# Half of one batch's queries transposed by a DMA instead of TensorE, and two scalars loaded from another queue

## The chip, the core and the metric

The kernel runs on one core of a Trainium2 chip. A core has five engines that run side by side and meet through semaphores: TensorE (PE in the profile; its weight loads are the rows PEld), VectorE (DVE), ScalarE (ACT), GpSimd (POOL) and SyncE (SP). Data comes and goes by DMA. Here GpSimd issues every load that turns float32 into bfloat16, and SyncE issues the rest: plain loads, stores, and DMAs that transpose.

The metric is the device time of one execution in microseconds. Before the change it is 219.6 (median of three runs, 218.88 to 221.15).

## The reference

Two parts follow each other: a block attention whose keys and values are mixed by a Sinkhorn-normalised matrix, and a feed-forward layer with a squared ReLU.

```python
# q, k, v: [4, 8, 768, 64]; sort_net: [4, 8, 8, 8]; 8 blocks of 96 tokens
P = sort_net
for _ in range(5):
    P = exp(P - max(P, -1));  P = P / sum(P, -1);  P = P / sum(P, -2)
k_sorted = einsum('bhij,bhjcd->bhicd', P, blocks(k))     # the same for v
attn = softmax(q_block @ k_sorted_block.T / sqrt(64))     # 96 x 96 a block
x = (attn @ v_sorted_block)  -> [3072 tokens, 512]

h = x @ w_in                                              # [512, 2048]
g = s * relu(h) ** 2 + b                                  # s, b scalars
out = g @ w_out                                           # [2048, 512]
```

## The kernel before

The work goes by batch (4) and by half batch (4 blocks of 96, 384 tokens, called TG); there are 8 half batches, t = 0 to 7. For each half batch and each pair of heads (hp = 0 to 3), `s_piece` or `s_banks` makes the scores and their exponential (tile `at`), `p_piece` multiplies by the values and divides (`x`), and `t_piece` (TensorE) or `t_dma` (a transposing DMA) turns `x` into `xt`. Then `ffn1` makes eight column groups (i = 0 to 7, 256 columns of w_in each): matmuls with w_in (L542, tile `hps`), ReLU on ScalarE (L556), the square on VectorE (L557). `ffn2` multiplies by w_out (L568, tile `ops`), and `store` (L593, L596) applies s and the bias and writes out. The bias, b times the column sums of w_out, is made once in `make_bias`: sixteen matmuls (L646, tile `cps`), four steps on VectorE (L648, L651), three copies on GpSimd (L654). No output can be stored before it.

The order on each engine is written by hand: the instructions of an engine run in the order of the program text (`manual_schedule`). `ffn1` and `ffn2` take dictionaries of slots: after column group i, or after a quarter of an output tile, the functions in that slot are emitted, so that attention of the next half or batch lies between the matmuls of the feed-forward layer.

What matters here is the beginning, where weights, keys, values and queries of the first two batches are loaded while the first half batches are computed.

- **GpSimd's queue** (L149 to L183): queries of batch 0, half 0 (`load_qh(0, 0)`, L106); keys of batch 0; then w_in in pieces (L142): four column groups c = 0 to 3 of 256 columns, each as four loads of 64 KB, and two groups of 512 columns as four loads of 128 KB each, used by the column groups 4 and 5, and 6 and 7; before c = 3 stand the queries of batch 0, half 1, as four loads (`load_qh(0, 1, 4)`, L167). Then w_out (L175), values of batch 1 (L95), some memsets, s and b (L181), keys of batch 1, and five of the eight row loads of batch 1's queries (L117). The three copies of the bias follow, and the last three row loads.
- **Queries of batch 0** come as `qh`: tokens as 64 groups of six, each group of a head a contiguous run of 384 numbers. `q_banks` transposes them on TensorE, 48 transposes of 64 x 64 for a half (L228, tile `tqb`), and ScalarE and VectorE move them into `qt` (L214, L216). The tokens of such a `qt` lie in the order (c, t), six apart, so the scores are written permuted and the exponential (L467) puts them back. `q_banks(0, 0)` runs before the first scores; `q_banks(0, 1)` stands in slot 0 of `ffn1(0)` (`QF0`, L694), and the first scores of half 1 (`SB(0)`, L462) in slot 2.
- **Queries of batches 1 to 3** come as rows of tokens (`load_q_rows`, tile `qtok`: 96 tokens on partitions, one load a block, runs of 64 numbers) and are transposed by a DMA on SyncE's queue (`q_dma`, L525), one for each half. Nothing is permuted then.
- The tiles `qh` and `qtok` share two buffers (tag rawq), the two kinds of `qt` share two others (tag qt).
- In `ffn2(0)` the keys of batch 1 are sorted (L328, tile `tpp`) and moved out of PSUM by VectorE and ScalarE (L216, L214, tile `ks`), and the values of batch 1 likewise (L378, tile `tvp`).

Of the kernel before, what the change touches and what calls it, by code (L numbers as in the profile page):

```python
# [10 lines left out]
BF = mybir.dt.bfloat16  # L11
AF = mybir.ActivationFunctionType
# [10 lines left out]
def kernel(  # L23
# [12 lines left out]
    nc = tc.nc  # L36

    B, H, S, D = q.shape
    NB = sort_net.shape[-1]
    BLK = S // NB  # L40
    BH = B * H
    NHP = H // 2
# [3 lines left out]
    HB = NB // 2  # L46
# [3 lines left out]
    KR = GAP + C2  # L50
# [3 lines left out]
    scale = float(D) ** -0.5  # L54
# [6 lines left out]
    trp = ctx.enter_context(tc.tile_pool(name="trp", bufs=2))  # L61
# [11 lines left out]
    CQ = 6  # L73
# [6 lines left out]
    for c in range(0, C2, CV):  # L80
        nc.sync.dma_start(out=v0f[:, c:c + CV, :].rearrange("p c d -> p (c d)"),
                          in_=raw[2][0][:, c * D:(c + CV) * D])
# [3 lines left out]
    def load(t, b, parts=1, behind=None, rest=None):  # L86
        ti = rawp.tile([128, C2, D], BF, tag=f"raw{t}", name=f"raw{t}")
        RAW[t, b] = ti
        if behind is not None:
            nc.gpsimd.tensor_copy(out=ti[0:behind.shape[0], 0, 0:1], in_=behind)  # L90
        n = C2 // parts
        for c in range(0, C2, n):
            if rest is not None and c == 2 * n:
                after(rest)
            nc.gpsimd.dma_start(out=ti[:, c:c + n, :].rearrange("p c d -> p (c d)"),  # L95
                                in_=raw["qkv".index(t)][b][:, c * D:(c + n) * D])
# [3 lines left out]
    def load_qh(b, half, parts=1):  # L100
        if b not in QH:
            QH[b] = rawp.tile([128, H, CQ, D], BF, tag="rawq", name="qh")
        qv = q[b].rearrange("h (f p c) d -> f p h (c d)", f=2, c=CQ)
        for h in range(0, H, H // parts):
            hs = slice(h, h + H // parts)
            nc.gpsimd.dma_start(  # L106
                out=QH[b][half * 64:(half + 1) * 64, hs].rearrange("p h c d -> p h (c d)"),
                in_=qv[half][:, hs])

    QTOK = {}  # L110

    def load_q_rows(b, ns=range(NB)):
        if b not in QTOK:
            QTOK[b] = rawp.tile([BLK, NB, H, D], BF, tag="rawq", name="qtok")
        qv = q[b].rearrange("h (n t) d -> t n h d", n=NB)
        for n in ns:
            nc.gpsimd.dma_start(out=QTOK[b][:, n], in_=qv[:, n])  # L117
# [4 lines left out]
    KS = [const.tile([128, NG, 2, GAP], BF, name=f"ks{i}") for i in range(2)]  # L122
# [17 lines left out]
    def load_wi(f0, f1, al=None):  # L140
        al = slice(0, NHP) if al is None else al
        nc.gpsimd.dma_start(out=wi[:, al, f0:f1], in_=wiv[:, al, f0:f1])  # L142

    def fill_vs(i):
        nc.gpsimd.memset(VS[i][:, :, D:VW], 1.0)
        nc.gpsimd.memset(VS[i][32:GAP, :, D:VW], 0.0)
        nc.gpsimd.memset(VS[i][32:C2, :, D:VW], 1.0)
# [10 lines left out]
    s_bc = const.tile([128, 1], FP)  # L158
    b_bc = const.tile([128, 1], FP)
# [3 lines left out]
    W4 = d_ff // 4  # L163
    W8 = d_ff // 8
    for c in range(4):
        if c == 3:
            load_qh(0, 1, 4)  # L167
        for a in range(NHP):
            load_wi(c * W8, (c + 1) * W8, slice(a, a + 1))
    for c in range(2, 4):  # L170
# [6 lines left out]
    nc.gpsimd.memset(VP[1][:, :, C2:GAP], 0.0)  # L177
    nc.gpsimd.memset(KS[1][:, :, :, C2:GAP], 0.0)
    fill_vs(1)
    for t, src in ((s_bc, moe_s), (b_bc, moe_b)):  # L180
        nc.gpsimd.dma_start(out=t, in_=src.to_broadcast([128, 1]))  # L181
    load("k", 1, 6)
    load_q_rows(1, range(NB - 3))  # L183

    rstat = const.tile([BH, NB], FP)
    rrec = const.tile([BH, NB], FP)
# [20 lines left out]
        else:  # L207
            eng.tensor_copy(out=o, in_=i)

    QT = {}  # L210

    def evac(eng, out, in_):
        if eng == "A":
            nc.scalar.copy(out=out, in_=in_)  # L214
        else:
            nc.vector.tensor_copy(out=out, in_=in_)  # L216

    def q_banks(b, half, engs):
        if b not in QT:
            QT[b] = trp.tile([128, 2, NHP, CQ, 64], BF, tag="qt", name="qt")  # L220
        pr = slice(half * 64, (half + 1) * 64)
        for u in range(2):
            tr = psb.tile([128, 1024], BF, tag="b", name="tqb")
            for a in range(2 * u, 2 * u + 2):
                for c in range(CQ):
                    for e in range(2):
                        o = (a % 2 * CQ + c) * 64
                        nc.tensor.transpose(out=tr[e * 64:(e + 1) * 64, o:o + 64],  # L228
                                            in_=QH[b][pr, 2 * a + e, c, :],
                                            identity=ident[pr, pr])  # L230
            evac(engs[u], QT[b][:, half, 2 * u:2 * u + 2].rearrange("p a c t -> p (a c t)"),
                 tr[:, 0:2 * TG])
# [3 lines left out]
            out=jsel, in_=ident.rearrange("p (h j z) -> p j h z", h=H, j=NB), axis=AX.XY, op=ALU.add),  # L236
        lambda: nc.vector.tensor_reduce(
            out=bm.rearrange("p (e z a) -> p e z a", e=2, z=2),
            in_=idv.rearrange("p a e j z -> p e z a j"), axis=AX.X, op=ALU.add),
# [190 lines left out]
    def s_piece(b, half, hp, sc=None):  # L430
        g0 = hp * NB + half * HB
        if sc is None:
            sc = psa.tile([128, 2, 512], FP, tag="a", name="sc")
        byp = len(QT[b].shape) == 5
        for n in range(HB):
            for e in range(2):
                pr = slice(e * 64, (e + 1) * 64)
                if byp:
                    o = sc[:, e, 0:TG].rearrange("p (c t) -> p c t", c=CQ)[:, :, 16 * n:16 * n + 16]
                    r = QT[b][pr, half, hp, :, 16 * n:16 * n + 16]  # L440
                else:
                    o = sc[:, e, n * BLK:(n + 1) * BLK]
                    r = QT[b][pr, half * HB + n, hp, :]
                nc.tensor.matmul(out=o, lhsT=KS[b % 2][pr, g0 + n].rearrange("p z c -> p (z c)"),  # L444
# [10 lines left out]
    def s_banks(b, half, hp):  # L455
        g0 = hp * NB + half * HB
        at = atp.tile([KR, 2, TG], BF, tag="at", name="at")
        sc = [psb.tile([128, TG], FP, tag="b", name="scb") for _ in range(2)]
        for n in range(HB):
            for e in range(2):  # L460
                pr = slice(e * 64, (e + 1) * 64)
                nc.tensor.matmul(  # L462
                    out=sc[e].rearrange("p (c t) -> p c t", c=CQ)[:, :, 16 * n:16 * n + 16],
                    lhsT=KS[b % 2][pr, g0 + n].rearrange("p z c -> p (z c)"),
                    rhs=QT[b][pr, half, hp, :, 16 * n:16 * n + 16], start=True, stop=True)
        for e in range(2):
            nc.scalar.activation(out=at[:, e].rearrange("p (t c) -> p t c", c=CQ),  # L467
                                 in_=sc[e][0:KR].rearrange("p (c t) -> p t c", c=CQ),
                                 func=AF.Exp, scale=scale)
        AT[b, half, hp] = at  # L470
# [62 lines left out]
    def part(t, i, hpl, fill=0):  # L533
        if (t, i) not in H1:
            H1[t, i] = psa.tile([128, 2, 512], FP, tag="a", name="hps")
        for j in range(fill):
            nc.tensor.matmul(out=H1[t, i][:, j % 2, TG:512], lhsT=zeros[:, 0:128],
                             rhs=zeros[:, 0:128], start=True, stop=True)
        for f in range(2):
            for hp in hpl:  # L540
                fc = (2 * i + f) * 128
                nc.tensor.matmul(out=H1[t, i][:, f, 0:TG], lhsT=wi[:, hp, fc:fc + 128],  # L542
                                 rhs=XT[t][:, :, hp, :],
                                 start=(hp == 0), stop=(hp == NHP - 1))

    def ffn1(t, slots, done={}, pre={}):

        gt = gtp.tile([128, NF, TG], BF, tag="gt", name="gt")
        GT[t] = gt
        for i in range(NF // 2):  # L550
            part(t, i, range(done.get(i, 0), NHP))
            for p in pre.get(i, ()):
                p()
            rt = rtp.tile([128, 2, TG], BF, tag="rt", name="rt")
            h = H1.pop((t, i))[:, :, 0:TG]
            nc.scalar.activation(out=rt, in_=h, func=AF.Relu)  # L556
            nc.vector.tensor_tensor(out=gt[:, 2 * i:2 * i + 2, :], in0=rt, in1=rt, op=ALU.mult)  # L557
            for p in slots.get(i, ()):
                p()
        XT.pop(t)  # L560
# [43 lines left out]
    k_banks(0, 2 * CK, "DA")  # L604
    v_piece(0, 0, "D")
    s_banks(0, 0, 0)
    s_piece(0, 0, 1)
    v_piece(0, CK, "D")
# [45 lines left out]
            nc.gpsimd.tensor_copy(out=bias[r:r + 32], in_=bias[0:32])  # L654
        load_q_rows(1, range(NB - 3, NB))

    def QF0(): return lambda: q_banks(0, 1, "AD")
    def SB(i): return lambda: s_banks(0, 1, i)
    def K(b, i, eng): return lambda: k_piece(b, i * CK, eng)
    def KP(b, i, engs="DA"): return lambda: k_pairs(b, i * CK, engs)  # L660
# [3 lines left out]
    def P(b, h, i): return lambda: p_piece(b, h, i)  # L664
    def TP(b, h, i, eng): return lambda: t_piece(b, h, i, eng)
# [7 lines left out]
    def halves(n):  # L673
# [16 lines left out]
        if n + 1 < B:  # L690
            s1[7 if n == 1 else 1] = [PDB(n + 1)]
        return s0, s1

    ffn1(0, {0: [QF0()], 2: [SB(0)], 3: [P(0, 1, 0), SB(1)], 4: [P(0, 1, 1), SB(2)],  # L694
             5: [P(0, 1, 2), SB(3)],
             6: [TP(0, 1, 0, "A"), TP(0, 1, 1, "D"), P(0, 1, 3)], 7: [TP(0, 1, 2, "A")]},
         {0: 3, 1: 3})
    part(1, 0, (0, 1))
# [14 lines left out]
    for b in range(1, B):  # L713
        n = b + 1
# [44 lines left out]
```

## Time and profile before

| what | us |
|---|---|
| median of three runs | 219.6 |
| the profiled execution, whole | 219.21 |
| its span, first to last instruction | 217.4 |
| TensorE busy | 208.7 |
| VectorE busy | 124.6 |
| ScalarE busy | 114.6 |
| GpSimd busy | 71.0 |
| matmuls with w_in (L542, 512 of them) | 86.7 |
| matmuls with w_out (L568) | 81.7 |
| transposing DMA of half a batch's queries, issue to landing (L525, 6 of them) | 3.8 to 9.5, median 7.2 |
| row load of queries, issue on GpSimd (L117, 24 of them) | 0.80 mean |

A row of the timeline gives the start, the length, the engine, the line, the operation, the tiles (out<-in), the shapes and the number of merged instructions; in brackets the idle time of the engine before it and what ended it. A row of the chain gives start, length and what. The chain follows the last instruction back, at each step to whatever released it; "issue" is time in which an engine waited for nothing that the profile shows. DMA share is the busy time of the core's 16 DMA engines as a share of the stretch; packets overlap, so it can pass 1. Busy rows of TensorE overlap too: a matmul's row is longer than its distance to the next.

### The profile page before, as it was taken

The numbers are of one execution on the slowest core, as the hardware profiler recorded it, in microseconds if no ns is written. First come the engines' busy times: TensorE is split into PE (matmuls) and PEld (weight loads), VectorE is DVE, ScalarE is ACT, GpSimd is POOL, SyncE is SP. The second block draws the span as 40 slices with busy tenths as digits, with TensorE's granted clock in tenths as the row PEclk, the third lists the DMA queues.
The fourth block names the chain that finished last, engine by engine and source line by source line (L and its number), as shares of the span: only waits on it lengthen the run. The fifth ranks groups of instructions, "written<-read, shape, count | busy, mean of one in ns | idle before, by whom it ended". The sixth has DMA issues, their size and how long they took to land.

```text
span 217.4 us, 5268 instructions
## 1 busy us (share of the span) xinstructions
PE 208.7 (96%) x2197; PEld 122.9 (57%) x2216; DVE 124.6 (57%) x259; ACT 114.6 (53%) x162; POOL 71.0 (33%) x129
## 2 busy tenths in 40 slices
PE   7988999999889999999999999999999999999994
PEld 5877666655345555655445556565455565654454
DVE  6777447538796986447637585448328544442122
ACT  4688687658877336664642447665360456650000
POOL 7659772659926022930032209500000000000000
PEclk9999999999999999999999999999999999999999
DMA  6999999999989959999999686999911450001212
GB/s 154 282 169 128 111 177 187 206 179 133 132 123 214 156 132 164 185 140 104 125 226 175 133 169 122 204 129 128 175 71 60 112 124 0 0 0 50 98 48 97
DMA packets 68023, 28.92 MB, mean 133 GB/s; under 512 B 51872, under 2 KB 64288, under 8 KB 68000
## 3 DMA queue, kind: packets, MB, share of 16 engines
q0 software_dynamic: 31168, 12.85, 51.5%
q1 hardware_dynamic: 36832, 15.74, 38.2%
q8 instruction: 17, 0.28, 0.6%
q14 instruction: 6, 0.05, 0.1%
HBM read 28.85 MB, written 7.86 MB: 169 GB/s over the span
## 4 chain that ended last, share of the span: by engine, by line
PE 70%; DMA 17%; POOL 8%; issue 2%; DVE 2%; DVEq 0%; POOLq 0%
PE ops L568 32%; PE hps L542 29%; DMA rawk<-in_k_dram 5%; DMA rawv<-in_v_dram 5%; DMA wo<-in_moe_w_out_dram 4%; PE pv L489 3%; DMA wi<-in_moe_w_in_dram 3%; PE sc L444 2%; POOL wi L142 2%; DVE ks L216 2%; POOL qtok L117 2%; PE ops L585 2%; POOL qh L106 1%; POOL bias L654 1%; PE tpp L328 1%
## 5 line engine op out<-in xcount | busy, mean ns | idle before, releaser
L542 PE MATMUL hps<-xt,wi 128*128 128x384 bf16 x512 | 86.7, 326 | 0.2 <-DVE rec L494 0.2
L568 PE MATMUL ops<-wo,gt 128*128 128x512 bf16 x350 | 81.7, 379 | 1.9 <-issue 1.3
L556 ACT ACTIVATE rt<-hps 128x768 bf16<-128x768 f32 x64 | 51.8, 811 | 30.6 <-PE hps L542 29.4
L542 PEld LDWEIGHTS <-wi 128*128 128x128 bf16 x512 | 48.7, 98 | 32.7 <-issue 1.3
L557 DVE TENSOR_TENSOR gt<-rt 128x768 bf16<-128x768 bf16 x64 | 35.5, 558 | 40.4 <-ACT rt L556 40.3
L568 PEld LDWEIGHTS <-gt 128*128 128x128 bf16 x368 | 33.9, 98 | 36.7
L593 DVE SCALAR_TENSOR_TENSOR ot<-ops,s_bc,bias 128x512 f32<-128x512 f32 (+2 forms) x27 | 18.6, 691 | 25.6 <-PE ops L568 21.9
L452 ACT ACTIVATE at<-sc 112x768 bf16<-112x768 f32 x24 | 17.8, 808 | 26.9 <-PE sc L444 26.9
L495 DVE TENSOR_TENSOR x<-pv,rec 96x512 bf16<-96x512 f32 x32 | 22.0, 687 | 1.1
L117 POOL DMA_DIRECT2D qtok<-in_q_dram x24 | 18.6, 800 | 2.6 <-DMA rawk<-in_k_dram 1.4
L489 PEld LDWEIGHTS <-at 112*128 112x128 bf16 (+1 forms) x256 | 12.4, 101 | 5.7 <-ACT vs L214 0.2
L214 ACT CAST ks<-tpp 64x512 bf16<-64x512 f32 x18 | 13.0, 724 | 4.6 <-DVE ks L216 4.1
L142 POOL DMA_DIRECT2D wi<-in_moe_w_in_dram x24 | 12.9, 571 | 4.6 <-DMA rawk<-in_k_dram 3.0
L489 PE MATMUL pv<-vs,at 112*128 112x66 bf16 (+1 forms) x256 | 13.3, 195 | 0.2 <-ACT vs L214 0.2
L216 DVE CAST ks<-tpp 64x512 bf16<-64x512 f32 x18 | 13.1, 726 | 0.3
L494 DVE RECIPROCAL rec<-pv 96x8 f32<-96x8 f32 x32 | 6.4, 199 | 11.6 <-PE pv L489 11.4
L95 POOL DMA_DIRECT2D rawk<-in_k_dram x21 | 11.2, 545 | 3.9 <-issue 2.0
L95 POOL DMA_DIRECT2D rawv<-in_v_dram x18 | 9.7, 563 | 5.3 <-DMA wo<-in_moe_w_out_dram 4.6
L132 PE MATMUL z<-zeros 128*64 128x80 bf16 (+2 forms) x123 | 9.8, 257 | 1.3 <-DVE zeros L120 1.2
L132 PEld LDWEIGHTS <-zeros 128*64 128x64 bf16 (+1 forms) x124 | 7.6, 134 | 3.0 <-DVE zeros L120 1.2
L90 POOL COPY rawv<-qt 128x1 bf16<-128x1 bf16 x2 | 0.4, 188 | 21.8 <-DMA qt<-qtok 21.8
L214 ACT CAST vs<-tvp 64x512 bf16<-64x512 f32 (+1 forms) x10 | 5.9, 585 | 2.1 <-PE tvp L378 2.0
(101 smaller groups left out, 135.5 us busy)
## 6 DMA issues: line engine op xcount, KB each, us to landing
out_dram<-ot SPq DMA_DIRECT2D x22, 256.0 KB, 2.8
rawv<-in_v_dram POOLq DMA_DIRECT2D x18, 128.0 KB, 6.4
rawk<-in_k_dram POOLq DMA_DIRECT2D x18, 128.0 KB, 4.4
qtok<-in_q_dram POOLq DMA_DIRECT2D x24, 96.0 KB, 6.1
wo<-in_moe_w_out_dram POOLq DMA_DIRECT2D x4, 512.0 KB, 10.2
v0f<-in_v_dram SPq DMA_DIRECT2D x4, 384.0 KB, 5.8
vd<-rawv SPq DMA_DIRECT2D x8, 192.0 KB, 5.3
vs<-vd SPq DMA_DIRECT2D x4, 384.0 KB, 7.5
```

The costliest lines, as they stand in the source:

```text
L95: nc.gpsimd.dma_start(out=ti[:, c:c + n, :].rearrange("p c d -> p (c d)"), in_=raw["qkv".index(t)][b][:, c * D:(c + n) * D])
L117: nc.gpsimd.dma_start(out=QTOK[b][:, n], in_=qv[:, n])
L214: nc.scalar.copy(out=out, in_=in_)
L216: nc.vector.tensor_copy(out=out, in_=in_)
L452: nc.scalar.activation(out=at, in_=sc[0:KR, :, 0:TG], func=AF.Exp, scale=scale)
L489: nc.tensor.matmul(out=pv[0:m, e, n * VW:(n + 1) * VW], lhsT=atf[:, c0:c0 + m], rhs=VS[b % 2][:, e * NG + g(n), :], start=True, stop=True)
L495: nc.vector.tensor_tensor(out=x[:, :, hp * 128:(hp + 1) * 128].rearrange("p n (e d) -> p e n d", e=2), in0=pvv[:, :, :, 0:D], in1=rec.unsq ...
L542: nc.tensor.matmul(out=H1[t, i][:, f, 0:TG], lhsT=wi[:, hp, fc:fc + 128], rhs=XT[t][:, :, hp, :], start=(hp == 0), stop=(hp == NHP - 1))
L556: nc.scalar.activation(out=rt, in_=h, func=AF.Relu)
L557: nc.vector.tensor_tensor(out=gt[:, 2 * i:2 * i + 2, :], in0=rt, in1=rt, op=ALU.mult)
L568: nc.tensor.matmul(out=ops, lhsT=gt[:, f, m * 128:(m + 1) * 128], rhs=wo[:, f, :], start=(f == 0), stop=(f == NF - 1))
L593: nc.vector.scalar_tensor_tensor(out=ot[:, ns], in0=ops, scalar=s_bc, in1=BIAS[0][:, ns], op0=ALU.mult, op1=ALU.add)
```

## The change

Half 1 of batch 0's queries is loaded as four row loads (blocks 4 to 7) in place of `load_qh(0, 1, 4)`, and one column group of w_in earlier (before c = 2). A transposing DMA on SyncE's queue, the first instruction there after the loads of the kernel's start, writes them into the second half of batch 0's `qt`, which is now taken from its pool at the start. `q_banks(0, 1)` goes from slot 0 of `ffn1(0)`, with its 48 transposes and two evictions. The scores of half 1 read the new layout and the exponential loses its permutation.

The loads of s and b leave GpSimd's queue. After column group 5 of `ffn1(0)`, VectorE clears each tile with a memset, and SyncE loads it once that memset is done.

```diff
     for c in range(4):
-        if c == 3:
-            load_qh(0, 1, 4)
+        if c == 2:
+            load_q_rows(0, range(HB, NB))
         for a in range(NHP):
             load_wi(c * W8, (c + 1) * W8, slice(a, a + 1))
...
-    for t, src in ((s_bc, moe_s), (b_bc, moe_b)):
-        nc.gpsimd.dma_start(out=t, in_=src.to_broadcast([128, 1]))
     load("k", 1, 6)
     load_q_rows(1, range(NB - 3))
+
+    qt0 = trp.tile([128, 2, NHP, CQ, 64], BF, tag="qt", name="qt")
+    Q1 = qt0[:, 1].rearrange("p a c t -> p (a c t)").rearrange("p (n a t) -> p n a t", n=HB, a=NHP)
+    nc.sync.dma_start_transpose(out=Q1.rearrange("p n a t -> p (n a) t"),
+                                in_=QTOK.pop(0)[:, HB:NB].rearrange("p n h d -> p (n h d)"))
...
-    QT = {}
+    QT = {0: qt0}
...
     def q_banks(b, half, engs):
-        if b not in QT:
-            QT[b] = trp.tile([128, 2, NHP, CQ, 64], BF, tag="qt", name="qt")
...
-                nc.tensor.matmul(
-                    out=sc[e].rearrange("p (c t) -> p c t", c=CQ)[:, :, 16 * n:16 * n + 16],
-                    lhsT=KS[b % 2][pr, g0 + n].rearrange("p z c -> p (z c)"),
-                    rhs=QT[b][pr, half, hp, :, 16 * n:16 * n + 16], start=True, stop=True)
+                if half == 0:
+                    o = sc[e].rearrange("p (c t) -> p c t", c=CQ)[:, :, 16 * n:16 * n + 16]
+                    r = QT[b][pr, half, hp, :, 16 * n:16 * n + 16]
+                else:
+                    o = sc[e][:, n * BLK:(n + 1) * BLK]
+                    r = Q1[pr, n, hp, :]
+                nc.tensor.matmul(out=o, lhsT=KS[b % 2][pr, g0 + n].rearrange("p z c -> p (z c)"),
+                                 rhs=r, start=True, stop=True)
         for e in range(2):
+            if half == 1:
+                nc.scalar.activation(out=at[:, e], in_=sc[e][0:KR], func=AF.Exp, scale=scale)
+                continue
...
-    def QF0(): return lambda: q_banks(0, 1, "AD")
+    def load_sb():
+        for t, src in ((s_bc, moe_s), (b_bc, moe_b)):
+            nc.vector.memset(t, 0.0)
+            nc.sync.dma_start(out=t, in_=src.to_broadcast([128, 1]))
...
-    ffn1(0, {0: [QF0()], 2: [SB(0)], 3: [P(0, 1, 0), SB(1)], 4: [P(0, 1, 1), SB(2)],
-             5: [P(0, 1, 2), SB(3)],
+    ffn1(0, {2: [SB(0)], 3: [P(0, 1, 0), SB(1)], 4: [P(0, 1, 1), SB(2)],
+             5: [P(0, 1, 2), SB(3), load_sb],
```

## The prediction

> **What bounds the kernel now.** I read the page first (busy shares), then the chain of waits that ended last, in order of time, then the timeline of TensorE, the loads one by one, and busy time by stretches.
>
> ```profile
> span 217.4 us, 5268 instructions
> PE 208.7 (96%) x2197; PEld 122.9 (57%) x2216; DVE 124.6 (57%) x259; ACT 114.6 (53%) x162; POOL 71.0 (33%) x129
> ```
>
> TensorE is busy for 96% of the span, so only its own work or its few waits can be won. The chain tells where those waits come from (start, length, what):
>
> ```profile
> 17.22 2.43 POOL qh L106 x4
> 19.65 2.15 POOL wi L142 x4
> 21.80 0.27 issue
> 22.07 6.14 DMA wi<-in_moe_w_in_dram
> ...
> 48.60 0.28 issue
> 48.88 0.53 POOL rawk L95
> 49.41 3.86 POOL qtok L117 x5
> 53.27 0.86 POOL bias L654
> ...
> 59.97 0.74 DVE ks L216
> 60.71 0.14 issue
> 60.85 0.41 PE tvp L378 x16
> ```
>
> Until 61 us the chain runs through GpSimd's queue of loads, to the copies of the bias (L654), the first output (L593) and, behind that on VectorE, the evictions of the keys (L216). After 61 us it is TensorE almost alone (L568, L542), so whatever the change shifts must be decided by then. GpSimd's pace is visible here too: the load at 22.07 starts 0.28 after the query load of 17.17 landed (21.79), the one at 48.88 starts 0.28 after the V load of 38.79 landed. In both pairs the earlier load is the eighth before the later one: eight loads are in flight at most.
>
> TensorE in the same stretch:
>
> ```profile
> 25.28 0.95 PE L228 MATMUL tqb<-ident,qh 64*64 64x64 bf16 x48
> 26.16 1.80 PE L542 MATMUL hps<-xt,wi 128*128 128x384 bf16 x10
> 27.89 0.34 PE L462 MATMUL scb<-qt,ks 64*128 64x96 bf16 x8
> 28.16 1.47 PE L542 MATMUL hps<-xt,wi 128*128 128x384 bf16 x8
> ...
> 30.17 1.48 PE L542 MATMUL hps<-xt,wi 128*128 128x384 bf16 x8
> ...
> 57.85 0.41 PE L378 MATMUL tvp<-pd,vp 64*128 64x64 bf16 x16 [0.70 <-DVE ks L216]
> ...
> 60.85 0.41 PE L378 MATMUL tvp<-pd,vp 64*128 64x64 bf16 x16 [0.42 <-DVE ks L216]
> ```
>
> From 25 to 57 us one row follows the other; then it waits twice for the key evictions, 0.70 + 0.42 = 1.12 us in all.
>
> **Transposes taken off TensorE.** The 48 transposes run from 25.28 to the next row's 26.16: 0.88 us come off a stretch where TensorE has no gap. The two evictions that go (ScalarE 0.79, VectorE 0.55) are beside the path: both engines wait for TensorE around them. The scores of half 1 now read and write runs of 96 and the exponential loses its permutation; 8 such matmuls took 0.34 permuted (27.89) and 0.34 in runs (batch 2, 113.99), and a 768-wide exponential 0.81 permuted (L448) and 0.81 plain (L452): nothing.
>
> **Row loads on GpSimd.** Four query loads (2.43 in all) become four row loads, which took 0.77 to 0.80 each at L117: 3.1, so +0.7. They move ahead of four 64 KB loads of w_in. The first 128 KB load of w_in loses its 0.27 wait, since the eighth before it is now a w_in load that landed; it starts 0.4 later. The displaced 64 KB loads start up to 3.1 later, at 18.2 to 19.8, and with their 2.8 to 3.2 to landing are there by 23; their matmuls run from 26.5. Covered by 3 us.
>
> In flight the rows are little dearer than what they replace: 18.60 to 21.60, full of 768-byte pieces, moved 133 GB/s at a DMA share of 1.02, and 51.50 to 55.50, full of 128-byte pieces, 126 GB/s at 1.91. The rate is the same; that the share is nearly double speaks for rival 2. [...]
>
> **The DMA transpose, on SyncE.** Its queue is empty but for this, so it delays nobody there. The rows take the place of the w_in loads after 15.10 (the first of five, from 14.57, ends there), one every 0.78; the last starts at 17.4 and lands 3.9 later (as the fourth row load of batch 1 did): 21.3. From issue to landing such a transpose took 3.8 with the loads quiet (61.73), 5.5 beside three row loads (55.69), and 9.5 at most, beside the V reads. The w_in loads here are like the middle one: I take 5.5, landing at 26.8. The scores want it at 27.89 - 0.88 = 27.0. So it hides, by 0.2; the ends are 25.1 and 30.8, a wait of 0 or 3.8.
>
> **What the transpose does to the loads behind it.** Beside the one at 55.69 a row load took 5.0 to landing, against 3.5 just before: 1.5 lost. Here it falls on the 128 KB loads of w_in. But 23.50 to 26.50 moved only 75 GB/s at a DMA share of 0.81, against 1.16 in 27.00 to 33.00: 3 x 0.35 / 1.16 = 0.9 us of room. So the queue behind moves by 0.4 + 1.5 - 0.9 = 1.0 us. The ends are 0.4 (all of the transpose in that room) and 1.9 (none). Who is next? The matmuls at 30.17 want the fourth 128 KB load at their fourth, 30.17 + 3 x 0.163 = 30.66; it landed at 23.63 + 6.5 = 30.1. With +1.0 it lands at 31.1, and TensorE, which would have come 0.88 earlier, waits: the gain of the transposes is gone and TensorE stands 0.5 later than before.
>
> **s and b.** Off GpSimd's queue, two issues of 0.54 go and every later load moves up two places among the eight. The 1.50 wait at 43.93 stays, for a K load. Two loads earlier, the second row load of batch 1 takes the start at 48.88 (still held by the V load), and the fifth row load ends at 48.88 + 4 x 0.78 = 52.0, where it ended at 53.27: -1.3 for the bias copies. Less 1.0 for the queue, the bias comes 0.3 earlier. VectorE's own work on the bias, which waited 3.27 for b (L648 at 49.05), starts near 46 and is no longer in the way. On SyncE the two broadcasts follow two memsets on VectorE (0.07 for the one at L188), after its part of the sixth column group, at about 36 us; the small sort-net load took 1.5 to landing, an output store beside full queues 5.6 (68.15): 38 to 42, where the bias wants them at 45.3. Past that, VectorE waits as before, up to 3.3 us, still beside the path.
>
> **The sum.** The chain bias, first output, key evictions, TensorE at 60.85 moves by 1.0 - 1.3 = -0.3. TensorE alone, +0.5 with 1.12 of waits to fill, comes 0.6 earlier: the chain decides. 219.21 (217.4 of span and 1.8 around it) - 0.3 = 218.9. That execution lay 0.4 under the median of 219.6, so on the median's scale 219.3. With the queue's ends, 0.4 and 1.9: -0.9 to +0.6, 218.7 to 220.2.
>
> **Rivals.** (1) The transpose lands late, and TensorE waits at the scores: slower. For it: four of the six such transposes of queries took 7 us or more, and four kept SyncE 4.3 to 6.3 us in the issue. Against: those ran beside the V reads, which are absent here. At 9.5 TensorE waits 3.8, less 0.88 and 1.12 of later waits filled: +1.8, 221.4. It turns from gain to loss at 0.88 + 1.12 = 2.0 of wait, that is from 7.7 to landing. Beyond this, a TensorE left idle may come back slower: the granted clock is 1.00 throughout and the longest wait of TensorE 1.2 us, so no row shows it; were as long a stretch as the wait run at half clock, half of it, 1.9 more: 223.3. [...]
>
> (2) The whole queue slides: the transpose takes its full share, and rows run slower than at L117. 0.4 + 1.9 (from 57 to 60 its packets took 65% of the engines) + 0.4 for the rows = 2.7, so 2.7 - 1.3 = +1.4: 221.0. For it: DMA share is 1.1 to 1.25 from 27 to 50. Against: the room at 23.5.
>
> (3) Both gains are kept: queue shift at 0, TensorE 0.88 + 1.12 = 2.0 earlier at most, the chain 1.3 earlier: 217.6 to 218.3. For it: the slow stretch 23.50 to 26.50 may not recur. Against: 0.4 of GpSimd issue is certain.
>
> **Chances.** Forecast 0.47; (1) 0.28, of it 0.17 over 1% (2.2 us, about what a measurement here tells from no change; landing past 9.9, or the clock); (2) 0.14, of it 0.04 over 1%; (3) 0.11, of it 0.05 under -1%. So faster 0.05, slower 0.21, the same 0.74. The range runs from inside (3), 218.0, to the middle of (1), 222.3.
>
> **What would show it.** Right: no tqb rows near 25 us, the transpose landing at 26 to 27, a wait of TensorE at the matmuls with the second half of w_in (near 30 us), the bias copies at about 53.0, the two waits for key evictions still there. Wrong: TensorE waiting for qt at its first scores of half 1 over 2 us, a granted clock under 1 behind it, or bias copies later than 53.3.

## The result and the profile after

The changed kernel took 222.47 us (median of six runs, 221.09 to 222.93), the kernel before 218.76 in the same comparison (six runs): a ratio of 1.0156 with a 95% interval of 1.0125 to 1.0187. It is slower, and outside the range forecast. (Each ratio here and below leaves out executions over 1.5% above the fastest of their kernel, and is against the kernel before in the same comparison, so it need not be the ratio of the medians.) The profiled execution of after took 222.93, its span 220.9, which is 3.5 more than the 217.4 of before.

The page of after, the span, the busy times, and two rows of the 40 slices (busy tenths of TensorE, and its granted clock):

```profile
span 220.9 us, 5177 instructions
...
PE 207.8 (94%) x2149; PEld 121.5 (55%) x2168; DVE 124.2 (56%) x260; ACT 114.3 (52%) x161; POOL 71.2 (32%) x127
...
PE   7788849999999999999999999999999999999994
...
PEclk9999988999999999999999999999999999999999
```

TensorE's busy time fell by 0.9 us, and the span rose all the same. (That fall is not the 0.88 of the 48 transposes alone: by the two pages of the profile the warm-up, L132, took 8.6 instead of 9.8, and the matmuls with w_in 87.7 instead of 86.7.) The slice with the 4 (27.6 to 33.1 us) is a hole that before did not have, and in two slices the clock is below 0.9. The chain of waits, in order of time (start, length, what), says what the hole waited for:

```profile
15.11 3.10 POOL qtok L117 x4
18.20 2.12 POOL wi L142 x4
20.33 1.54 DMA wi<-in_moe_w_in_dram
21.86 9.00 DMA qt<-qtok
30.87 0.04 issue
30.91 0.34 PE scb L469 x8
31.26 2.17 PE hps L550 x8
```

The row loads cost 3.10 on GpSimd, as forecast (3.1); the last rows landed at 21.78 and the transpose was issued at 21.86, 0.5 to 0.6 later than the 21.3 forecast. Then the transpose took 9.00 from issue to landing, and from there the chain is TensorE alone. The timeline of TensorE beside it, and its busy time by stretches (the columns: stretch, length, busy time and instructions of TensorE, granted clock, DMA share, GB/s):

```profile
24.04 2.84 PE L550 MATMUL hps<-xt,wi 128*128 128x384 bf16 x16
30.91 0.34 PE L469 MATMUL scb<-qt,ks 64*128 64x96 bf16 x8 [4.04 <-DMA qt<-qtok]
31.19 2.24 PE L550 MATMUL hps<-xt,wi 128*128 128x384 bf16 x8
33.23 0.67 PE L497 MATMUL pv<-vs,at 112*128 112x66 bf16 x8
```

```profile
28.00:31.00 3.00, 0.09 (x4) 1.00 1.37 162
31.00:33.00 2.00, 2.00 (x16) 0.69 1.23 201
33.00:35.00 2.00, 2.00 (x21) 0.50 1.24 202
35.00:37.00 2.00, 2.00 (x26) 0.96 1.24 206
```

The first scores of half 1 waited 4.04 us. The eight matmuls behind them, 1.47 in the profile of before, took 2.24: the granted clock was 0.5 from 31.75, 0.84 after the scores had begun, to 35.16, that is for 3.41 us. This is the case that the forecast told of but could show with no row of before. How long a wait it takes is not shown here: e8 and e9 below came to half clock after waits of 1.75 and 1.20 at the longest, and e2 stayed at 1.00 after 3.23.

The later rows of GpSimd and TensorE answer to those that the forecast of no change rested on:

```profile
50.12 3.86 POOL L117 DMA_DIRECT2D qtok<-in_q_dram  x5 [0.42 <-PE cps L654]
53.97 2.43 POOL L662 COPY bias<-bias 32x512 f32<-32x512 f32 x3
```

```profile
58.26 3.40 PE L576 MATMUL ops<-wo,gt 128*128 128x512 bf16 x15 [0.16 <-PE tpp L329]
61.59 0.41 PE L379 MATMUL tvp<-pd,vp 64*128 64x64 bf16 x16
```

The bias copies came at 53.97 instead of 53.26, later, not earlier. But nobody waits for them now: TensorE is so late that the key evictions are done when it gets there, and the two waits at L378, 0.70 and 0.42, are gone.

A table of lags shows where the time came from and what gave some of it back. It takes the start of the same piece of work in each trace (a ReLU of the first half batch, column groups 2 and 4; the second output tile; the first ReLU of batch 1), less the start in the trace of before:

| piece, and its start before | after | e1 | e2 | e3 | e4 | e6 | e11 | e12 |
|---|---|---|---|---|---|---|---|---|
| group 2, 27.99 | -1.08 | -0.18 | -1.04 | -0.94 | -0.26 | -0.17 | -0.20 | -0.81 |
| group 4, 31.68 | +4.52 | -0.18 | +2.20 | +0.74 | +3.46 | -0.17 | -0.20 | -0.81 |
| second output, 60.73 | +2.96 | -1.27 | +0.63 | -0.06 | +1.89 | -1.17 | -1.60 | -1.67 |
| batch 1, 79.96 | +3.15 | -0.70 | +0.83 | +1.42 | +2.10 | +2.55 | -1.23 | +0.20 |
| end, 217.44 | +3.50 | -0.33 | +1.27 | +1.75 | +2.45 | +3.06 | -1.24 | +1.54 |

For after: the scores stand 3.0 late (30.91 against 27.89, the 0.88 of the transposes already taken off), the half clock adds 1.5, the waits that TensorE had later take back 1.56, batch 1 adds 0.2 and the last microsecond 0.35.

### The profile page after: what moved, and what is told of

The parts are those of the page before. It is cut to its first block, busy times and chain, and to the rows that moved or that the text cites. A ratio compares the mean times of both kernels' runs of the same rounds, so it can differ in the third digit from the quotient of the medians.

```text
span 220.9 us, 5177 instructions
## 1 busy us (share of the span) xinstructions
PE 207.8 (94%) x2149; PEld 121.5 (55%) x2168; DVE 124.2 (56%) x260; ACT 114.3 (52%) x161; POOL 71.2 (32%) x127
## 4 chain that ended last, share of the span: by engine, by line
PE 84%; DMA 10%; POOL 3%; issue 1%; DVE 0%; POOLq 0%
PE hps L550 37%; PE ops L576 36%; DMA rawk<-in_k_dram 5%; DMA qt<-qtok 4%; PE pv L497 4%; PE sc L445 2%; PE ops L593 2%; POOL qtok L117 1%; POOL wi L142 1%; PE tpp L329 1%; DMA wi<-in_moe_w_in_dram 1%; PE scb L469 1%; PE tvp L379 1%; PE tvr L404 1%; POOL rawk L95 0%
## 5 line engine op out<-in xcount | busy, mean ns | idle before, releaser
L550 PE MATMUL hps<-xt,wi 128*128 128x384 bf16 x512 | 87.7, 329 | 0.2 <-DVE rec L502 0.2
L453 ACT ACTIVATE at<-sc 112x768 bf16<-112x768 f32 x24 | 17.8, 809 | 26.6 <-PE sc L445 26.6
L117 POOL DMA_DIRECT2D qtok<-in_q_dram x28 | 21.7, 790 | 1.3 <-issue 0.6
L95 POOL DMA_DIRECT2D rawk<-in_k_dram x21 | 11.2, 541 | 4.3 <-DMA wo<-in_moe_w_out_dram 2.5
L132 PE MATMUL z<-zeros 128*64 128x80 bf16 (+2 forms) x123 | 8.6, 237 | 1.3 <-DVE zeros L120 1.2
L132 PEld LDWEIGHTS <-zeros 128*64 128x64 bf16 (+1 forms) x124 | 6.5, 116 | 2.9 <-DVE zeros L120 1.2
L469 PE MATMUL scb<-qt,ks 64*128 64x96 bf16 x56 | 2.7, 215 | 4.5 <-DMA qt<-qtok 4.0
```

What stands on the lines that cost most here:

```text
L132: nc.tensor.matmul(out=z[0:m, 0:w], lhsT=zeros[:, 0:m], rhs=zeros[:, 0:w], start=True, stop=True)
L453: nc.scalar.activation(out=at, in_=sc[0:KR, :, 0:TG], func=AF.Exp, scale=scale)
```

## The experiments

Theory 1: the transpose lands late, TensorE waits and comes back at half clock; that is the whole loss. Theory 2: it is the loads that the rows and the transpose hold up. A third question came up on the way: why the transpose took 9.0.

**e1, the loads of s and b alone.** The kernel before with only that part of the change.

```diff
-    for t, src in ((s_bc, moe_s), (b_bc, moe_b)):
-        nc.gpsimd.dma_start(out=t, in_=src.to_broadcast([128, 1]))
...
-             5: [P(0, 1, 2), SB(3)],
+             5: [P(0, 1, 2), SB(3), load_sb],
```

> Only the loads of s and b are moved; the queries are as before. Theory A (the loss of the whole change is TensorE's wait for the transposed queries and the half clock behind it): this part gains or does nothing. The bias copies come up to 1.3 us earlier, the two waits of TensorE for the key evictions (0.70 and 0.42) go, so 0.5 to 1.1 us under the kernel before, ratio 0.995 to 0.998. Rival B (moving s and b itself costs, by a late landing on SyncE's queue or by what the K loads do two places earlier): slower than before by 0.5 us or more.

Measured: 218.88 us (12 runs), ratio 0.9983 (0.9959 to 1.0008); no difference that can be told. By the trace the part does what the forecast said of it: the bias copies start at 52.21, 1.05 earlier (1.3 forecast), the key waits go, and TensorE is 1.27 earlier at 61 us. Half of it is lost again at the second query transpose of batch 1, and 0.37 at the very end. What TensorE waited behind that transpose (what, total, times, longest):

```profile
PE sc L442 <- DMA qt<-qtok: 0.4, 1, 0.4
```

**e2, the queries alone.** The changed kernel with the loads of s and b back on GpSimd.

```diff
+    for t, src in ((s_bc, moe_s), (b_bc, moe_b)):
+        nc.gpsimd.dma_start(out=t, in_=src.to_broadcast([128, 1]))
...
-             5: [P(0, 1, 2), SB(3), load_sb],
+             5: [P(0, 1, 2), SB(3)],
```

> Only the queries are changed; s and b stay on GpSimd's queue. Theory A: the wait for the transposed queries is as long as in the changed kernel (about 4 us at the first scores of half 1), so its time, 222 to 223. Rival B (s and b carry a good part of the loss): 221 or less.

Measured: 221.28 us, ratio 1.0097 (1.0063 to 1.0131). The loss is in the part with the queries. In its profiled execution the transpose took 8.25 and TensorE waited 3.23, but the clock stayed at 1.00, and the eight matmuls behind kept their 1.47:

```profile
30.14 0.34 PE L471 MATMUL scb<-qt,ks 64*128 64x96 bf16 x8 [3.23 <-DMA qt<-qtok]
30.42 1.47 PE L552 MATMUL hps<-xt,wi 128*128 128x384 bf16 x8
```

That execution took 220.5. Of the others of this kernel three, with a mean clock of 0.989 to 0.992, took 221.03 to 221.41, and one with 1.0 took 221.59, so here the clock does not order them. In after it does: its one run with the clock at 1.0 throughout took 221.09, the others, at 0.985 to 0.992, 221.81 to 222.93. But a low mean clock is no mark of this change alone: of 65 executions of the kernel before in the comparisons of these experiments, 15 had a mean clock of 0.990 to 0.992 too, and no trace shows where.

**e3, no wait for the transpose.** The scores of half 1 read a tile of zeros instead of the transposed queries, so the scores of that half are left out of what is computed; all loads and the transpose remain.

```diff
-                    r = Q1[pr, n, hp, :]
+                    r = zeros[pr, n * BLK:(n + 1) * BLK]
```

> The whole change, but the scores of half 1 read a tile of zeros instead of the transposed queries (left out: those scores). All loads and the transpose still run, TensorE need not wait for them. Theory A: the wait of 4.0 us and the half clock are gone, and what the transpose does to the loads of w_in is left: the fourth wide load lands 1.1 us later than before, TensorE waits for it some 0.6 us, two later waits are filled: 218 to 219, at most 0.5 us over the kernel before. Rival C (the loss is the delay of all loads behind the transpose): 221 or more.

Measured: 221.11 us, ratio 1.0111 (1.0058 to 1.0165). Theory 1 as it stood falls: with no wait at the scores and a clock of 1.0, most of the loss is there all the same. The waits of TensorE in this trace:

```profile
PE hps L550 <- DMA wi<-in_moe_w_in_dram: 1.2, 3, 0.5
...
PE sc L445 <- DMA qt<-qtok: 0.7, 1, 0.7
...
PE hps L550 <- DMA xt<-x: 0.5, 1, 0.5
```

Freed from one wait, TensorE runs into the next DMA: the 128 KB loads of w_in, then the transposes of batch 1's queries and of its `X`. The first of these is the wait that the forecast had named; TensorE is 0.74 late at 31.68, where 0.5 was forecast.

**e4, the hole filled.** Seventeen matmuls of zeros in front of the first scores of half 1, so that TensorE isn't idle.

```diff
-    ffn1(0, {2: [SB(0)], 3: [P(0, 1, 0), SB(1)],
+    ffn1(0, {2: [lambda: warm(17), SB(0)], 3: [P(0, 1, 0), SB(1)],
```

> The whole change, with 17 matmuls of zeros of 512 columns (3.7 us at 0.216 each) ahead of the first scores of half 1, so that TensorE is busy while it waits. Theory A with the clock as part of the loss: the start of the scores does not move (30.9 us), the granted clock stays at 1.00, and the time falls by 1.4 to 1.7 us, to 220.8 to 221.1. Rival D (the clock's dip is beside the path, or it comes from something other than the idle TensorE): same time as the changed kernel within 0.5 us, or the dip stays.

Measured: 221.4 us, ratio 1.0103 (1.0058 to 1.0148), and a clock of 0.998 to 1.0 in all four runs.

```profile
27.53 3.83 PE L132 MATMUL z<-zeros 128*128 128x512 bf16 x17
31.29 0.45 PE L469 MATMUL scb<-qt,ks 64*128 64x96 bf16 x8
31.68 1.48 PE L550 MATMUL hps<-xt,wi 128*128 128x384 bf16 x8
```

The scores come 0.4 later than in after (31.29), the matmuls behind keep 1.48, and the ratio falls from after's 1.0156 to 1.0103, some 1.1 us. The two intervals overlap, so the totals alone don't show that difference. The lag table shows the step: from the scores to group 4 after loses 1.5 (3.0 to 4.5), e4 0.06 (3.40 to 3.46), and at the end they are 1.05 apart. So the half clock is a cause of its own, worth about 1 us of the 3.7 by these two traces; the rest stays without it.

**e5 and e6, the rows earlier.** The row loads before the first (e5) or the second (e6) column group of w_in instead of the third.

```diff
-        if c == 2:
+        if c == 0:    # e5;  c == 1 in e6
             load_q_rows(0, range(HB, NB))
```

> The changed kernel, with the row loads of batch 0 placed before the first column group of w_in instead of the third, so that rows and transpose start about 6 us earlier. If the late landing is the whole cause (theory 1): rows landed by 16 to 17, transpose landed by 21 to 26 even at its dearest 9.0 to 9.5 us, no wait of TensorE at the scores of half 1 and a clock of 1.0; TensorE 0.9 early until the next wait, and 219 us or less (217.8 to 219.2). If what it costs is the loads that a transpose and the rows hold up, wherever they lie (theory 2, as in the run whose scores didn't wait and still took 221.1): no wait at the scores, but one of 1 to 2 us at the matmuls with w_in between 26 and 34, and 220.5 to 221.5.

> The same with the row loads before the second column group, some 3 us earlier than in the changed kernel. Theory 1: transpose issued near 18.5, landed between 24 and 27.5, wait at the scores 0 to 0.6, clock 1.0, 218 to 219.5. Theory 2: 220.5 to 221.5 with the wait at w_in.

Measured: e5 221.73 us, ratio 1.012 (1.0059 to 1.0182); e6 222.61 us, ratio 1.0104 (1.002 to 1.0189). In e6 the transpose was issued at 18.33, took 7.10 and landed at 25.43; no wait at the scores, none at w_in, and at 61 us TensorE was 1.17 ahead of before. Up to there theory 1 holds, and neither e5 nor e6 has the wait at w_in that theory 2 asked for. Then everything was lost between 64 and 80 us. The chain of e6 there:

```profile
62.54 4.99 DMA qt<-qtok
67.54 0.05 issue
67.58 0.34 PE sc L445 x8
...
72.96 7.12 DMA xt<-x
80.09 0.14 issue
80.22 1.46 PE hps L550 x8
```

In before the second query transpose of batch 1 took 3.81 and the first transpose of an `X` 4.27; here they took 4.99 and 7.12. In before that `X` landed at 77.25 and its first matmul began at 77.67, which is 0.4 of slack (a row of SyncE's timeline in before, and one of TensorE's):

```profile
72.98 1.95 SPq L515 DMA_TRANSPOSE xt<-x  x1
77.67 1.47 PE L542 MATMUL hps<-xt,wi 128*128 128x384 bf16 x8
```

So a lead that TensorE wins before 61 us passes this place only as far as these transfers let it: e6 kept nothing of 1.17, e1 kept 0.70 of 1.27, and e11 below, where the query transpose took 3.83, kept 1.23 of 1.60. e5 was 3.2 late already at group 2: TensorE had gaps of 1.31 and 1.94 before 25 us in which it waited for nothing that the profile shows, and then a granted clock of 0.5 from 26.07 to 29.48.

**e7, the 128 KB loads of w_in held back** until the transpose has landed, by a copy on GpSimd that reads one of its elements.

```diff
+    scr0 = const.tile([128, 1], BF)
+    nc.gpsimd.tensor_copy(out=scr0, in_=Q1[:, HB - 1, NHP - 1, 0:1])
     for c in range(2, 4):
```

> The changed kernel, with the 128 KB loads of w_in held back by a one-element copy on GpSimd that reads the transposed queries, so that nothing large is in flight beside the transpose after the 64 KB loads. Not meant to be fast: TensorE will wait for w_in instead. It measures the transpose: if the 128 KB loads made it 9.0 us long (theory: shared DMA engines), it takes 4 to 5.5 from issue to landing; if it is slow by itself here (a stretch of slow DMA at 24 to 27 that the kernel before has too), it takes 8 to 9 all the same.

Measured: 225.66 us (one run), and 5.96 for the transpose: neither 4 to 5.5 nor 8 to 9. With the 128 KB loads in flight it took 5.83 (e3) to 9.00 (after), so one sample can't tell what part is theirs. That stays open; but the halt of packets told of next is in this trace too, from 24.94 to 26.75, so it doesn't need those loads.

**The long packets.** In some of the long transposes packets of 256 bytes, 18 to 31 ns for the middle half of them in after, take over 1000 ns and all end at one moment; in others they don't (the 7.31 of before, issued at 104.26, has none over 227 ns). In after, from 25.1 on, all packets in flight ended together at 26.6; in the stretch from 23 to 27 us (40 slices of 0.1 us) next to nothing moves meanwhile, the loads included. The rows are GB/s, and the queue that carries instructions:

```profile
GB/s 128 138 148 113 146 123 90 95 95 126 120 159 143 161 159 143 115 251 120 141 179 143 115 69 41 18 5 8 8 8 10 10 8 10 10 51 233 282 282 282
...
q8 instruction: 1, 0.02, 1.5%
```

That one packet on the instruction queue is 16 KB and started at 24.71, 0.4 us before the halt. Before and after have 17 of these each; counted against TensorE's own instructions, matmuls and weight loads, in before they come after 254, 568, 859 and so on up to 4234, that is one for every 249 on average (249 in after too; the 4413 instructions of before's page over 17 are 260). So they look like TensorE's code, fetched block by block. That is the author's reading: a row gives the queue, the size and the time, not what was fetched. A fetch below is one of these transfers. Single distances lie between 155 and 314 in before and between 135 and 337 in after, and in e8 the first came after 384, so such a count can't place a fetch to the microsecond. Taking 96 instructions off TensorE near 25 us moved the fetches behind: the next two came at 33.69 and 46.58 in before and at 42.13 and 55.00 in after, 8.4 later, where TensorE's work itself was 4.5 late. The next three experiments are meant to move the fetches alone, with the warm-up's multiplications by zeros; theory F is that a fetch beside a transpose holds it up.

**e8, e9, e10, the fetches moved** in the kernel before, in e6 and in after.

```diff
-    warm(102, 80, 64)
+    warm(54, 152, 64)     # e8 on before, e9 on e6: 96 instructions less
+    warm(174, 47, 64)     # e10 on after: 144 more
```

> The kernel before, with one thing altered: 48 fewer and wider multiplications by zeros in the warm-up of TensorE (54 of 152 columns for 102 of 80), so that 96 instructions less stand ahead of everything else on TensorE, as in the changed kernel. The trace has 17 transfers of 16 KB on an instruction queue, one for about every 256 instructions of TensorE; with 96 less they fall later, by the trace near 64 and 74 us instead of 60.6 and 70.5, that is into the second query transpose of batch 1 (61.7 to 65.5) and the first transpose of an X (73.0 to 77.3). Theory F (a code fetch 1 to 3 us after a transpose's issue holds it up): one of these takes 4.4 to 5.5 instead of 3.8 and 4.3, with packets of 1000 ns and more, and the span is 0.2 to 2 us longer. Theory N (the fetch is a bystander): 3.8 and 4.3 stay, 219.3 us within 0.3%.

> The kernel with the row loads before the second column group (e6), with the same 96 instructions less in the warm-up, so that by its trace the code fetches fall near 24.4, 53, 69.7 and 82 us and none beside the first query transposes (18.3, 62.5) or the first X transpose (73.0), where e6 had one each at 20.2, 63.8 and 75.6. Theory F: these take 5 to 6.5, 3.8 and 4.3 instead of 7.1, 5.0 and 7.1, the wait for the X transpose (2.4) goes, and the time is 218 to 219.5. Theory N: as e6, waits for qt and xt of some 3 us together, 220.5 to 222.5.

> The changed kernel with 72 more and narrower multiplications in the warm-up (174 of 47 columns for 102 of 80): 144 more instructions, so that by its trace the code fetch at 24.7 comes near 19 and the next near 36, and none lies beside the first transpose (21.9). Theory F: the transpose takes 6 to 7 instead of 9.0, TensorE waits 1 to 2 at the scores instead of 4.0, clock 1.0 throughout, 219.5 to 221. Theory of the loads alone (the 128 KB loads of w_in share the engines with it): 8 to 9 as before, a wait of 3 to 4, 221.5 to 222.9.

Measured: e8 220.69 us, ratio 1.0066 (1.0031 to 1.01); e9 220.84 us, ratio 1.007 (1.0031 to 1.0108); e10 221.55 us, ratio 1.0112 (1.0052 to 1.0173). The fetches and the transposes did not meet as they were meant to, so the totals tell little of theory F. In e8 the fetches came near the times worked out, at 64.67 and 73.85, but that is 3.2 after the one transpose's issue and 0.4 before the other's; they took 3.9 and 3.8, and the test wasn't one. In e10 a fetch came at 23.79, still beside the transpose, which took 6.43. In e9 the two transposes after 60 us were free of fetches, and took 3.80 and 3.87 where e6 had 4.99 and 7.12: that e6 lost 3.7 between 61 and 80 us, and e9 only 0.15, goes the way of theory F. But e9 was 0.72 late at 61 us, where e6 was 1.17 ahead, so e9 had no lead to lose there, and this alone could explain part of it.

What took the time in these three is another thing. The timelines of TensorE, e8 first, then e10:

```profile
16.59 0.37 PE L346 MATMUL tkb<-pd,rawk 128*64 128x64 bf16 x5 [1.17 <-issue]
```

```profile
17.18 0.66 PE L357 MATMUL tv<-pd,vp 128*64 128x64 bf16 x29 [1.48 <-issue]
...
22.15 0.41 PE L357 MATMUL tv<-pd,vp 128*64 128x64 bf16 x14 [1.91 <-issue]
```

TensorE stands still with nothing to wait for, in the middle of equal instructions. Between 11 and 23 us it uses up some 250 short instructions in 3.5 to 5 us, and its gaps begin 0.4 to 1.2 us after the start of a fetch (14.2 in e8; 14.8 and 19.8 in e10). The kernel before has a gap too, of 0.53 at 17.1, but that began 2.2 after its fetch. That these are waits for code is the author's reading; no semaphore or row shows it. In e8 the granted clock was 0.50 from 14.08 to 20.91 as well, before and around the gap, after a wait of 1.75 for the Sinkhorn part that ended at 11.2; so its loss has two parts, which no run separates. In e9 it was 0.50 from 13.26 to 16.68. Together, in e8, 1.3 us of span hang on how many trivial instructions stand ahead.

Over all 14 profiles, the second query transpose of batch 1 and the transposes of `X` whose landing is on record, taken where less than 20 KB of loads started from 1 us after their issue on: 61 had no fetch between 0.5 and 2.8 us after their issue and took 3.84 in the median; 12 had one and took 4.68 (3.96 to 5.19). With loads beside them and no fetch: 5.4 (4.24 to 6.35, 16 of them). The window was chosen after looking at the traces. Clearer is the second query transpose of batch 1 alone, one in each profile and none with a load beside it. In seven a fetch started 1.2 to 3.0 us after its issue, and they took 4.42 to 5.24; the other seven, e8 with its fetch at 3.2 among them, took 3.77 to 3.91. This too is a pattern, and no experiment has set a fetch on purpose beside an otherwise quiet transpose.

**e11, the order at the end.** At the end of the program SyncE goes through the semaphores of its transfers one by one, some 0.06 us each where it need not wait, in the same order in before and in after. In before the last store had the one that comes last; the transfers added on SyncE (three in after, two in e1) shift it to the third place in after and the second in e1 of eight, and the rest is gone through after the store has landed. From that semaphore to the end of the span: 0.91 in before, 1.22 in after, 1.28 in e1. The kernel of e1 with six more loads of four bytes:

```diff
             nc.sync.dma_start(out=t, in_=src.to_broadcast([128, 1]))
+        for i in range(6):
+            nc.sync.dma_start(out=sn2[i], in_=sort_net.rearrange("b h i j -> (b h) i j")[0:1, 0, 0:1])
```

> The kernel of e1 (s and b by SyncE, nothing else) with six loads of four bytes more on SyncE behind them, so that the number of SyncE transfers added is eight and the last store gets the semaphore that SyncE waits for last at the end, as before. If the order of these waits is what e1 lost at its end: from the last store's landing to the end of the span 0.9 as before instead of 1.3, and 218.2 to 218.7 us. If not: 1.3, as e1 (ratio 0.998).

Measured: 0.90 from that semaphore to the end, as in before, so the 0.37 is explained. The time is 218.94 us (12 runs), ratio 0.9982 (0.9942 to 1.0021); the profiled execution took 218.31 and kept its lead to the end (-1.24 in the table), but the median is above what was expected. It is not shown to be faster than before.

**e12, all that was learnt put together:** e6 with 12 fewer warm-up multiplications and five small loads on SyncE.

```diff
-    warm(102, 80, 64)
+    warm(90, 91, 64)
...
+        for i in range(5):
+            nc.sync.dma_start(out=sn2[i], in_=sort_net.rearrange("b h i j -> (b h) i j")[0:1, 0, 0:1])
```

> An attempt at a version faster than both: the row loads before the second column group (e6), 12 fewer multiplications in the warm-up (90 of 91 columns for 102 of 80), and five loads of four bytes on SyncE so that the last store's semaphore is waited for last again. By e6's trace the code fetches then fall near 21.1, 27.8, 52.6, 66.1 and 77.0 us: one still beside the first query transpose of batch 0, none in the first 3 us of the second of batch 1 (62.5) or of the first X transpose (73.0). If fetches and the order at the end are what e6 lost after 61 us: transposes of 3.8 and about 4.3 there, the 1.2 us that e6 had won at 61 us is kept, and 217.8 to 218.8 us. If TensorE starves for instructions in the first 26 us (its gaps with nothing waited for were 1.5 in e6, 2.4 to 3.4 in e9 and e10): 219.5 to 221.5.

Measured: 221.64 us, ratio 1.0155 (1.0114 to 1.0197). TensorE was 1.67 ahead at 61 us, the largest lead of all, and 0.20 behind at 80. (At its very end VectorE stood still for 1.86 until an earlier store had landed, where it is 0.54 in before; that is the 1.3 between 80 us and the end.) The chain of e12:

```profile
61.99 4.68 DMA qt<-qtok
66.67 0.05 issue
66.72 0.34 PE sc L446 x8
...
72.10 5.65 DMA xt<-x
77.75 0.14 issue
77.88 1.46 PE hps L551 x8
```

The fetches fell at 63.52 and 74.56, beside both transposes, and not at 66.1 and 77.0 as worked out from e6. No version faster than the kernel before was found.

## Why the prediction was wrong

**The failed step** is "I take 5.5, landing at 26.8 [...] So it hides, by 0.2". In the ten profiles with this transpose it took 5.83 to 9.00, never 5.5; in after it took 9.00 and landed at 30.87. Of the 4.1 that this is late, 3.5 are the transpose and 0.6 its issue. So the term that was mis-sized is the transpose's time to landing, and the wait that was put at nothing measured 4.04. Why it took 9.0 stays open. The 5.5 came from one transpose of batch 1 beside row loads, the only one of six that lay beside loads and not beside the V reads, and a forecast that hides by 0.2 out of 5.5 hung on it. The forecast's upper end of 30.8 is where it landed; the weight on it was too small.

**The wait and the clock.** The first rival gave a wait of 3.8 and, with as long a stretch at half clock, 223.3. That is 3.7 over the median that it started from (219.6), and 3.7 was measured (222.47 less 218.76). Both parts were there: the wait was 4.04, and 3.41 us ran at 0.5. But no row of before shows a clock that halves behind a wait, nor for how long; the 1.9 was the author's assumption, and the runs showed in its place a half clock of 3.41 us in after, which cost 1.5, and no half clock behind the 3.23 of waiting in e2. That the sum fits so well is in part luck: the half clock cost 1.5 where it had 1.9, of later waits 1.56 were filled where it had 1.12, and it lacked the 0.2 at batch 1 and the 0.35 at the end.

**Transposes, rows, evictions.** -0.88 on TensorE, +3.1 on GpSimd: right. The row loads were judged by rate alone; from 17 to 20 us, full of 128-byte pieces, they moved 91 to 109 KB per us at a DMA share of 1.5 to 1.8, while the 512-byte pieces of w_in moved 140 at 1.2 just behind them. So pieces of 128 bytes were dearer here, though not twice as slow in rate, and the rows still landed by 21.78.

**The queue behind.** The fourth 128 KB load of w_in landed at 31.86 instead of 30.17: 1.7 later, where 1.0 was taken between 0.4 and 1.9. Its wait showed only in e3 (+0.74 at group 4, against +0.5 forecast), since the longer wait for the queries lay over it. The 0.9 of "room" at 23.5 to 26.5 was no room: while the transpose's packets ran or stood still, the loads moved 1.5 and 7 KB in whole microseconds (25 to 27). With s and b 1.05 earlier (e1) and the queue 1.7 later, the bias copies came 0.7 later, where the forecast had 0.3 earlier.

**s and b.** The gain of 1.3 was there (1.05 for the bias, 1.27 for TensorE in e1), s and b came in time, at 46.24 and 47.61 with the bias matmuls at 48.85, but two steps later it was not worth a measurable time. That the key waits were the last ones that matter ("whatever the change shifts must be decided by then", of 61 us) was wrong: the second query transpose and the `X` transpose of batch 1 stood behind them, the latter with 0.4 us of slack.

## What to carry to other kernels

A transfer that takes the place of work on the busiest engine has to land by the worst time that the trace shows for its kind, not by the time of the row that looks most alike; in after it came 4.04 us too late for TensorE, which then lost 1.5 more by its clock. Before counting a gain, look past the wait that it removes to the next transfers in the chain, and to how much slack each has. And a change in the number of instructions far ahead can move a microsecond in places that it doesn't touch: in e8 it was 1.3, of which a gap of 1.17 that looks like a wait for code and a stretch of 6.83 at half clock are parts that these runs don't separate.

## What was not expected of the hardware

A transposing DMA of half a batch's queries took 3.81 us with no load beside it (before, issued at 61.73), and up to 9.50 in before and 9.69 in after beside the V reads; while the packets of the first one in after ran, the loads on the other queue nearly stopped (1.5, 7 and 26 KB in the three microseconds from 25 to 28, 141 from 22 to 23). At times packets stood still together for over 1 us (1442 ns in after at 25.14; 3358 ns at most, in e6). Before 85 us there are 18 such halts (four packets or more of over 1000 ns) in the 14 profiles, and beside each a 16 KB transfer on the instruction queue started, at most 1.3 us before its first long packet or 0.9 after; but later, beside the V reads, they come without one so near: in before 18 packets of over 1000 ns from 102.22 on, 3.3 us after the last such transfer, and in e10 15 packets stood for 0.6 to 0.84 us until 77.0, 6 us after one. After 3.23 us of idle time the clock stayed at 1.00 in one execution of e2, and behind 4.04 it was at 0.50 in after; but e8 fell to 0.5 at 14.08, for 6.83 us, after no wait of TensorE longer than 1.75, and e9 at 13.26, for 3.41 us, after none longer than 1.2. So the length of a single wait doesn't tell when the clock falls here. What remains open is how much of the 9.0 is due to the fetch, to the loads beside it, and to chance.
